# Attention's diagonal term summed by TensorE from transposed k and r, with loads and weight parts re-timed

## The chip, the core and the metric

One NeuronCore of a Trainium2 chip runs the whole program. Its engines are PE (TensorE: matmuls and, as "PEld", the weight loads that go with them), DVE (VectorE), ACT (ScalarE), POOL (GpSimd) and SP (SyncE, which here issues nearly all DMAs). Each works off its own list of instructions in order and waits for others by semaphores. PE writes only to PSUM; DVE and ACT read PSUM. The metric is the device time of one execution in microseconds (us); lower is better.

## What is computed

An RWKV-like attention over 4 batches, 8 heads, 768 steps and 48 dimensions per head, and then a mixture of experts (8 experts, top 2) over the 3072 tokens that it yields. The part that the change touches is the attention:

```python
def _attn_ref(r, k, v, w, u):
    state = np.zeros((B, H, D, D), dtype=np.float32)
    for t in range(S):
        kt, vt, rt = (k[:, :, t], v[:, :, t], r[:, :, t])
        cur = np.einsum('bhd,bhe->bhde', u[None] * kt, vt)
        y[:, :, t] = np.einsum('bhd,bhde->bhe', rt, state + cur)
        state = w[None, :, :, None] * state + np.einsum('bhd,bhe->bhde', kt, vt)
```

The term with `cur` is, for each token and head, one number c = sum over d of r·u·k, times that token's v. Below it is the "u-term", and c is the tile `c8` (128 tokens by 8 heads).

## The kernel before

**Tiles.** The attention is cut into 24 tiles (`NT`) of 128 tokens: six chunks of time by four batches, batch innermost. One loop runs over the tiles i = 0 to 23; the expert part follows and has its own loops. The order of each engine's instructions is the order in which the Python code writes them (a manual schedule), so software pipelining is written by hand: iteration i of the loop finishes tile i and prepares tiles i+1 and i+2.

**One iteration.** POOL multiplies k by powers of w (`prep_k`, two halves of four heads, tile `kd`), and for the u-term r by k (`uterm_rk`) and the product by u (`uterm_u`, tile `rku`); it also scales the state (`zup_p`). PE multiplies keys with values (`kvup`, into `RV`), then builds the output in `yout`: from tile 4 on the state's part (`zb`), the router logits of tile i-1, and the masked scores `am` times v, all into one PSUM tile `py`. Next PE turns k and r of tile i+2 (`turn_kr`, into `KX` and `RV`), computes the scores of tile i+1 into `PAB`, and turns the finished output of tile i (`turn_x`). DVE reads `kvup`'s result (`zup_v`, tile `zt`), sums `rku` over d into `c8` (`uterm_b`), adds y and c·v into `x` (`xout`), scales the turned r (`rT`), and masks the scores (`mask`, two halves). ACT copies the turned k (`kT`), the turned x (`xT`), the state (`zb`) and the logits (`lg`), and, from tile 9 on, multiplies v by c head by head (`uterm_c`: `CV_EARLY` heads an iteration early, the rest in its own); up to tile 8 DVE does that in one instruction (`cv`).

**Between these** stand two more streams. `one_step` puts one or two small DVE instructions of the router (from iteration 8 on) at eight places of an iteration. And the first expert's weights (`w_split`) come in seven parts: a load of 512 or 384 KB into a staging tile `stg`, two ACT copies that round it (lines 344 and 347) and two DVE subtractions that keep the rest (lines 346 and 349). `W_LD` says at the end of which iteration a part is loaded, `W_AT0` from which iteration on it is split (three iterations each).

**Loads.** k and r of a tile are loaded six iterations ahead, v five ahead, all from SP, which also stores every x and loads the weight parts, in the order of the code. Buffers: 3 for `kd`, 6 each for k, r, v, 4 for x; one PSUM bank for `py`.

Two dependencies follow from the whole-tile bookkeeping of `py`: `lg` waits for the last matmul written to `py` before it in the code, and `xout` waits for `lg`.

Of the kernel before, what the change touches and what calls it, by code (L numbers as in the profile page):

```python
# [9 lines left out]
F32 = mybir.dt.float32  # L10
# [5 lines left out]
AF = mybir.ActivationFunctionType  # L16
# [12 lines left out]
XD2 = 4  # L29
FILL = 1  # L30
PVB = 4
CV_EARLY = 3
STEPS_P1 = 0.8
STEPS_P2 = 4.2
STEPS_R = 1.6
# [4 lines left out]
NK = 6  # L40
# [3 lines left out]
W_AT = ((3, 7, 8), (3, 5, 7, 9))  # L44
NOT = 4

W_LD = {1: 0, 3: 1, 5: 2, 7: 3, 9: 4, 11: 5, 14: 6}
W_AT0 = (4, 6, 8, 11, 13, 16, 18)


@with_exitstack
def kernel(
# [83 lines left out]

    per_dim(wp, w, (nc.sync, nc.scalar))
    per_dim(up, u, (nc.scalar, nc.scalar))
    kd = [att.tile([128, H, 64], F32, name=f"kd{j}", bufs=1) for j in range(3)]
    rd = [att.tile([128, H, 64], F32, name=f"rd{j}", bufs=1) for j in range(NK)]  # L140
    rt, kt, vt = {}, {}, {}

    def load(i, part=(0, 3)):
        c, b = divmod(i, B)
        for nm, src, dst in (("kt", k, kt), ("rt", r, rt), ("vt", v, vt))[part[0]:part[1]]:
            if nm == "rt":
                t = rd[i % NK][:, :, :D]
# [7 lines left out]
    load(0, (0, 2))  # L155
    load(1, (0, 2))
    load(0, (2, 3))
    ub = att.tile([128, H, D], F32, name="ub", bufs=1)
    load(2, (0, 1))
    load(1, (2, 3))  # L160
    load(2, (1, 3))
# [47 lines left out]
    nc.vector.tensor_mul(pwk[:, :, 96:128], pwk[:, :, 64:96], pwk[:, :, 95:96].to_broadcast([128, NP, 32]))  # L209
    nc.scalar.activation(pwr[:, :, 0:64], pwk[:, :, 127:63:-1], AF.Copy)  # L210
    w128 = const.tile([128, NP, 1], F32, name="w128")

    kT, rT = {}, {}
    def turn_rows(dst, o, src, base=0):
# [27 lines left out]
    pub = psum.tile([128, H, 64], F32, name="pub", tag="py0")
    for p in range(NP):
        nc.tensor.transpose(pub[:, 2 * p:2 * p + 2, :].rearrange("p a b -> p (a b)"),
                            up[:, p:p + 1].to_broadcast([128, 128]), ident)
    nc.scalar.activation(ub, pub[:, :, :D], AF.Copy)
# [133 lines left out]


    AM, X, CV, PY, PA = {}, {}, {}, {}, {}
    LG, XT, PL = {}, {}, {}

    KD = {}
    HALVES = (slice(0, H // 2), slice(H // 2, H))

    def prep_k(i):
        KD[i] = kd[i % 3][:, :, :D] if i else att.tile([128, H, D], F32, name="rku")
        for h in HALVES:  # L390
            nc.gpsimd.tensor_mul(KD[i][:, h], kt[i][:, h], tabk[:, h, :D])  # L391

    RKU, C8 = {}, {}

    def uterm_rk(i):
        RKU[i] = att.tile([128, H, D], F32, name="rku")
        for h in HALVES:
            nc.gpsimd.tensor_mul(RKU[i][:, h], rt[i][:, h], kt[i][:, h])

    def uterm_u(i):  # L400
        for h in HALVES:
            nc.gpsimd.tensor_mul(RKU[i][:, h], RKU[i][:, h], ub[:, h])

    def uterm_a(i):
        uterm_rk(i)
        uterm_u(i)

    def uterm_b(i):
        c8 = att.tile([128, H, 1], F32, name="c8", bufs=2)
        nc.vector.tensor_reduce(c8, RKU[i], AX.X, ALU.add)  # L410
        C8[i] = c8
        CV[i] = att.tile([128, H, D], F32, name="cv")
        if i <= GROUPS[0][1]:
            nc.vector.tensor_mul(CV[i], vt[i], c8.to_broadcast([128, H, D]))
# [6 lines left out]
    def turn_kr(i):  # L421
        if i >= NT:
            return
        for src, dst in ((kd[i % 3], KX), (rd[i % NK], RV)):
            for p in range(NP):
                turn_rows(dst, p * 64, pair(src, p))
        kT[i] = att.tile([128, NP, 128], F32, name="kT", bufs=2)
        nc.scalar.activation(by_row(kT[i]), halves_of(KX, 0, NP), AF.Copy)
        rT[i] = att.tile([128, NP, 128], F32, name="rT", bufs=2)
        nc.vector.tensor_mul(by_row(rT[i]), halves_of(RV, 0, NP), by_row(pwr))  # L430
        one_step()
# [58 lines left out]
    def yout(i):  # L490
        c, b = divmod(i, B)
        pyb = psum.tile([128, 512], F32, name="py", tag="py0")
        PL[i - 1] = pyb[:, DM:DM + LREP * 2 * E].rearrange("p (a e) -> p a e", e=2 * E)
        py = pyb[:, :DM].rearrange("p (h d) -> p h d", d=D)
        first = [True, True]

        def acc_mm(o, lhsT, rhs, q, last):
            qs = slice(q * 64, (q + 1) * 64)
            nc.tensor.matmul(o[qs], lhsT[:, qs], rhs, start=first[q], stop=last, skip_group_check=True)  # L499
            first[q] = False  # L500

# [619 lines left out]
    def tick():  # L1121
        for x in late_mm:
            x[0] -= 1
            if x[0] == 1:
                x[2]()
        while late_mm and late_mm[0][0] <= 0:
            late_mm.pop(0)[1]()
            credit[0] -= 0.25
        at_pe[0] = max(at_pe[0] - 1, 0)

    def one_step():
        k = 0
# [12 lines left out]

    consts_a()
    uterm_rk(0)
    prep_k(1)
    prep_k(0)
    uterm_u(0)  # L1150
    scores(0)
    mask(0)
    load(4)
    load(5, (0, 2))
    warm(WARM3)
    turn_kr(1)
    uterm_b(0)
    nc.vector.tensor_mul(w128, tmpw[:, :, 63:64], tmpw[:, :, 63:64])
    def rstep(us, lag=2):

# [53 lines left out]
                          zrow[:96, None, :].to_broadcast([96, 2, DM]))  # L1214

    def products(i):
        if i + 2 < NT:
            prep_k(i + 2)
        zup_p(i - 1)
        if i + 1 < NT:  # L1220
            uterm_a(i + 1)

    flag = consts_c()
    for i in range(NT):
        products(i)
# [315 lines left out]
```

## Time and profile before

| | |
|---|---|
| Time, median of 3 runs (lowest to highest) | 593.28 us (592.33 to 593.3) |
| The profiled execution, its own time | 594.2 us |
| Its span, first to last instruction | 592.5 us |
| Mean granted TensorE clock | 0.993 |
| PE busy over the span | 565.8 us (96%) |
| DVE, ACT, POOL busy | 359.4, 286.5, 274.0 us |

The profiled execution is 0.9 us above the median and has 1.7 us outside its span. In the slices of the page PE is busy nearly without a break in the expert part, from about 133 us on, where no line of the change runs; the first 133 us are the attention, where PE, DVE and the DMA queues are all busy between 80 and 100% and hand work to each other tile by tile.

### The profile page before, as it was taken

Reading aid. Unit: us, or ns where it says so; the run is one execution under the profiler, and the core shown is the slowest. Engines: PE = TensorE matmul, PEld = TensorE weight load, DVE = VectorE, ACT = ScalarE, POOL = GpSimd, SP = SyncE. Lnnn points to the kernel's source line nnn. Section 1 sums busy time; section 2 is a strip of 40 time slices with the busy share of each in tenths; the row PEclk is TensorE's granted clock in tenths of the full one; section 3 lists DMA queues with packets and bytes.
Section 4 is the critical chain, followed back from the end, with each engine's and each line's share of the span. In section 5 each row is a group of like instructions: output and inputs, shape, how many; then the busy total and the mean of one; then the engine's idle time right before and its main releaser. Section 6 shows DMA issues by size and latency. Waiting matters only on the chain.

```text
span 592.5 us, 13758 instructions
## 1 busy us (share of the span) xinstructions
PE 565.8 (96%) x5281; PEld 540.4 (91%) x5282; DVE 359.4 (61%) x866; ACT 286.5 (48%) x721; POOL 274.0 (46%) x420
## 2 busy tenths in 40 slices
PE   7897987889999999999999999999999999999995
PEld 5897886879999999999999999999999999999995
DVE  5998998977886554546455645555454546454331
ACT  4456786853362633554445554454545454445220
POOL 8987876721015543426333552344242526333222
PEclk9899999999999999999999999999999999999999
DMA  9989999429514643874655645464845555423211
GB/s 149 192 204 191 225 209 196 102 70 267 182 60 146 203 143 84 194 173 152 140 168 113 198 114 175 102 181 111 198 129 159 153 134 174 124 93 84 66 35 42
DMA packets 143016, 86.44 MB, mean 146 GB/s; under 512 B 118415, under 2 KB 133006, under 8 KB 142944
## 3 DMA queue, kind: packets, MB, share of 16 engines
q1 hardware_dynamic: 132384, 56.67, 40.6%
q0 software_dynamic: 9936, 28.83, 15.9%
q8 instruction: 43, 0.70, 0.5%
q14 instruction: 29, 0.24, 0.1%
q10 hardware_dynamic: 624, 0.00, 0.1%
HBM read 58.83 MB, written 19.76 MB: 133 GB/s over the span
## 4 chain that ended last, share of the span: by engine, by line
PE 79%; DVE 10%; DMA 5%; ACT 2%; POOL 2%; issue 2%; POOLq 0%; SPq 0%; ACTq 0%
PE ph L1044 35%; PE pym L1078 33%; PE py L499 2%; PE pym L1069 2%; PE pym L1071 2%; DVE am L451 2%; DMA stg<-in_moe_w_dram 2%; DVE x L518 2%; DVE rT L430 1%; DMA xg<-xd,GR 1%; DMA out_dram<-ot,TK 1%; PE KX L217 1%; DVE c L410 1%; PE py L527 1%; PE PAB L443 1%
## 5 line engine op out<-in xcount | busy, mean ns | idle before, releaser
L1078 PE MATMUL pym<-w1h,hb 128*128 128x384 f32 x768 | 200.6, 337 | 0.0
L1048 DVE SCALAR_TENSOR_TENSOR hb<-ph,hb 128x384 fp32r<-128x384 f32 (+1 forms) x136 | 72.5, 533 | 116.3 <-ACT ht L1046 68.4
L1044 PE MATMUL ph<-xh,w0h 128*128 128x384 f32 (+3 forms) x408 | 140.0, 344 | 0.0
L1078 PEld LDWEIGHTS pym<-w1h,hb 128*128 128x128 f32 x768 | 139.4, 188 | 0.3
L1044 PE MATMUL ph<-xh,w0l 128*128 128x384 f32 (+3 forms) x408 | 138.8, 341 | 0.0
L1044 PE MATMUL ph<-xl,w0h 128*128 128x384 f32 (+3 forms) x408 | 133.5, 341 | 0.0
L1078 PE MATMUL pym<-w1l,hb 128*128 128x384 f32 x384 | 129.5, 337 | 0.0
L1046 ACT ACTIVATE hb<-ph 128x384 fp32r<-128x384 f32 (+1 forms) x136 | 64.2, 472 | 107.7 <-PE ph L1044 105.0
L1101 POOL DMA_INDIRECT out_dram<-ot,TK x56 | 58.8, 1050 | 103.6 <-DVE ot L1097 52.6
L947 POOL DMA_INDIRECT xg<-xd,GR x56 | 61.2, 1092 | 70.6 <-DVE r_oa L636 18.8
L1044 PEld LDWEIGHTS ph<-xh,w0h 128*128 128x128 f32 x408 | 76.7, 188 | 3.3 <-ACT xh L987 0.2
L1044 PEld LDWEIGHTS ph<-xh,w0l 128*128 128x128 f32 x408 | 76.7, 188 | 2.6
L1044 PEld LDWEIGHTS ph<-xl,w0h 128*128 128x128 f32 x408 | 76.1, 188 | 2.8
L1078 PEld LDWEIGHTS pym<-w1l,hb 128*128 128x128 f32 x384 | 72.1, 188 | 0.1
L956 POOL DMA_INDIRECT pv<-out_dram,GA x49 | 49.8, 1016 | 48.2 <-DMA out_dram<-ot,TK 35.8
L1018 ACT ACTIVATE xh<-xj 128x384 fp32r<-128x384 f32 (+1 forms) x42 | 21.1, 502 | 43.5 <-DVE xj L1016 41.6
L1086 ACT ACTIVATE ot<-pym 128x384 f32<-128x384 f32 x39 | 19.0, 486 | 40.6 <-PE pym L1078 29.9
L1019 DVE TENSOR_TENSOR xl<-xj,xh 128x384 fp32r<-128x384 f32 (+1 forms) x42 | 22.4, 534 | 24.7 <-ACT xh L1018 13.6
L1004 ACT ACTIVATE pl<-xg 128x768 uint16<-128x768 uint16 (+1 forms) x42 | 35.3, 841 | 1.0 <-DMA xd<-pl 0.9
L391 POOL TENSOR_TENSOR kd<-kt,tabk 128x192 f32<-128x192 f32 x46 | 27.7, 624 | 12.8 <-PE RV L463 6.4
L451 DVE TENSOR_TENSOR am<-PAB,mneg 128x512 int32<-128x512 int32 x48 | 31.6, 680 | 1.9 <-PE PAB L443 1.8
L419 ACT ACTIVATE cv<-vt,c 128x48 f32<-128x48 f32 x120 | 30.2, 323 | 5.0 <-DVE c L410 2.6
(272 smaller groups left out, 827.3 us busy)
## 6 DMA issues: line engine op xcount, KB each, us to landing
stg<-in_moe_w_dram SPq DMA_DIRECT2D x24, 512.0 KB
stg<-in_moe_w_dram SPq DMA_DIRECT2D x32, 384.0 KB
rd<-in_r_dram SPq DMA_DIRECT2D x24, 192.0 KB
vt<-in_v_dram SPq DMA_DIRECT2D x24, 192.0 KB
xd<-x SPq DMA_DIRECT2D x24, 192.0 KB
out_dram<-ot SPq DMA_DIRECT2D x16, 288.0 KB
kt<-in_k_dram SPq DMA_DIRECT2D x23, 192.0 KB
xg<-xd,GR POOLq DMA_INDIRECT x56
```

The lines of the kernel that those rows point to most:

```text
L391: nc.gpsimd.tensor_mul(KD[i][:, h], kt[i][:, h], tabk[:, h, :D])
L419: nc.scalar.activation(CV[i][:, h, :], vt[i][:, h, :], AF.Copy, scale=C8[i][:, h, :])
L451: nc.vector.tensor_tensor(am[:, :, h].bitcast(I32), pa[:, :, h].bitcast(I32), mneg[:, None].to_broadcast([128, 2, NP // 2, 128]), op=ALU.b ...
L947: nc.gpsimd.indirect_dma_start(out=xg[:n], out_offset=None, in_=xd[:rows_of(early_)], in_offset=bass.IndirectOffsetOnAxis(ap=GR[:n, e * NJ ...
L956: nc.gpsimd.indirect_dma_start(out=pv[:n], out_offset=None, in_=out, in_offset=bass.IndirectOffsetOnAxis(ap=GA[:n, e * NJ + t:e * NJ + t + ...
L1004: nc.scalar.activation(pl[:n], XG[e, t][:n, :DM].bitcast(U16).rearrange("p (d two) -> p two d", two=2), AF.Copy)
L1019: nc.vector.tensor_sub(xl, xj, xh.bitcast(F32))
L1044: nc.tensor.matmul(ph[:, :w_], a[:, d, fs], x[:, d, :w_], start=(j == 0), stop=(j == len(q) - 1))
L1046: nc.scalar.activation(h_[:, f, 0, :], ph[:, a:b], AF.Relu)
L1048: nc.vector.scalar_tensor_tensor(h_[:, f, 1, :], ph[:, a:b], 0.0, h_[:, f, 0, :].bitcast(F32), op0=ALU.max, op1=ALU.subtract)
L1078: nc.tensor.matmul(py, hb[:, f, a, hs], x[:, f, :], start=(j == 0), stop=(j == len(q) - 1))
L1101: st = nc.gpsimd.indirect_dma_start(out=out, out_offset=bass.IndirectOffsetOnAxis(ap=TK[:n, q:q + 1], axis=0), in_=ot[:n], in_offset=None, ...
```

## The change

The u-term is computed from the transposed tiles instead. POOL multiplies `rT` by `kT` (128 partitions of two heads' dimensions, 4 pairs of heads by 128 tokens, two halves of 256 elements), and PE sums over the partitions: eight matmuls per tile with two columns each, whose moving operand is `uw`, a table of u times w by heads. The sum lands in a free corner of the PSUM tile `py`, and DVE copies its 8 columns to `c8`. The multiplication by u on POOL and the sum on DVE go, and with them the table `ub`.

```diff
-CV_EARLY = 3
+CV_EARLY = 2
+NKD = 4
-W_LD = {1: 0, 3: 1, 5: 2, 7: 3, 9: 4, 11: 5, 14: 6}
-W_AT0 = (4, 6, 8, 11, 13, 16, 18)
+W_LD = {1: 0, 4: 1, 6: 2, 9: 3, 11: 4, 14: 5, 16: 6}
+W_AT0 = (5, 8, 10, 13, 15, 18, 20)
...
     def uterm_a(i):
-        uterm_rk(i)
-        uterm_u(i)
-
-    def uterm_b(i):
-        c8 = att.tile([128, H, 1], F32, name="c8", bufs=2)
-        nc.vector.tensor_reduce(c8, RKU[i], AX.X, ALU.add)
-        C8[i] = c8
+        RK[i] = att.tile([128, NP, 128], F32, name="rk", bufs=2)
+        for h in (slice(0, NP // 2), slice(NP // 2, NP)):
+            nc.gpsimd.tensor_mul(RK[i][:, h], rT[i][:, h], kT[i][:, h])
+
+    def uterm_sum(i, pyb, alone):
+        c8 = pyb[:, CO:CO + H].rearrange("p (a s) -> p a s", s=2)
+        for p in range(NP):
+            for q in range(2):
+                qs = slice(q * 64, (q + 1) * 64)
+                nc.tensor.matmul(c8[qs, p, :], RK[i][:, p, qs], uw[:, p, :], start=alone, stop=True,
+                                 skip_group_check=True)
+        C8[i] = att.tile([128, H, 1], F32, name="c8", bufs=2)
         CV[i] = att.tile([128, H, D], F32, name="cv")
+        return lambda: nc.vector.tensor_copy(C8[i][:, :, 0], pyb[:, CO:CO + H])
+
+    def uterm_v(i):
         if i <= GROUPS[0][1]:
-            nc.vector.tensor_mul(CV[i], vt[i], c8.to_broadcast([128, H, D]))
+            nc.vector.tensor_mul(CV[i], vt[i], C8[i].to_broadcast([128, H, D]))
...
     def products(i):
-        if i + 2 < NT:
-            prep_k(i + 2)
-        zup_p(i - 1)
         if i + 1 < NT:
             uterm_a(i + 1)
+        zup_p(i - 1)
+        if i + 3 < NT:
+            prep_k(i + 3)
...
-        if i + 6 < NT:
-            load(i + 6, (0, 2))
+        if i + 5 < NT:
+            load(i + 5, (0, 2))
...
         yout(i)
+        if i + 1 < NT:
+            c8_out = uterm_sum(i + 1, PB[i], False)
...
-        if i + 5 < NT:
-            load(i + 5, (2, 3))
+        if i + 4 < NT:
+            load(i + 4, (2, 3))
...
         one_step()
         one_step()
+        uterm_v(i)
+        xout(i)
         if i + 1 < NT:
-            uterm_b(i + 1)
+            c8_out()
         one_step()
-        one_step()
-        xout(i)
         one_step()
...
             mask(i + 1)
             tick()
             one_step()
+            one_step()
```

On PE, at tile 4, the first with `zb` (names as in the text; `L499` with `zb` and with `am` and `L527` are `yout`, `L217` the turns, `L443` the scores, `L463` `kvup`), before:

```order
L463 MATMUL RV<-vt,kd_100 48x48 x8
L499 MATMUL py<-zb_212,rT 64x96 x8
L527 MATMUL py<-wg,xT 64x64 x6
L499 MATMUL py<-vt,am 64x48 x16
L217 MATMUL KX<-ident,kd_99 128x64 x8
L217 MATMUL RV<-ident,rd_102 128x64 x8
L443 MATMUL PAB<-rT,kT 128x128 x8
L217 MATMUL KX<-ident,x 128x64 x6
```

and after the change:

```order
L462 MATMUL RV<-vt,kd_99 48x48 x8
L499 MATMUL py<-zb_211,rT 64x96 x8
L527 MATMUL py<-wg,xT 64x64 x6
L499 MATMUL py<-vt,am 64x48 x16
L405 MATMUL py<-uw,rk 64x2 x8
L218 MATMUL KX<-ident,kd_101 128x64 x8
L218 MATMUL RV<-ident,rd_103 128x64 x8
L442 MATMUL PAB<-rT,kT 128x128 x8
L218 MATMUL KX<-ident,x 128x64 x6
```

The eight matmuls of the sum (`L405`) stand between `yout` and the turns, so everything behind them on PE comes later by their length, and they are now the last writes to `py` before `lg`.

On DVE, at tile 10 (`L410` is the sum over d, `L518` x, the lines `RT`, `r_d`, `r_s` are router steps, `w0l` a weight part's rest), before:

```order
L451 TENSOR_TENSOR am<-PAB,mneg 128x2x256
L561 SCALAR_TENSOR_TENSOR RT<-RT,r1r 128x64
L346 TENSOR_TENSOR w0l_505<-stg,w0h_504 128x512
L476 TENSOR_TENSOR zt<-RV,z_210 128x192
L561 SCALAR_TENSOR_TENSOR RT<-RT,r1r 128x64 x2
L410 TENSOR_REDUCE c_1434<-rku 128x8
L561 SCALAR_TENSOR_TENSOR RT<-RT,r1r 128x64
L563 SCALAR_TENSOR_TENSOR RT<-RT,r1s 128x64
L518 TENSOR_TENSOR x<-py,cv 128x384
L703 TENSOR_SCALAR RT<-RT 128x64
L430 TENSOR_TENSOR rT<-RV,pwr 128x2x4x64
```

and after the change:

```order
L450 TENSOR_TENSOR am<-PAB,mneg 128x2x256
L561 SCALAR_TENSOR_TENSOR RT<-RT,r1r 128x64 x2
L346 TENSOR_TENSOR w0l_519<-stg,w0h_518 128x512
L475 TENSOR_TENSOR zt<-RV,z_209 128x192
L561 SCALAR_TENSOR_TENSOR RT<-RT,r1r 128x64 x2
L518 TENSOR_TENSOR x<-py,cv 128x384
L409 COPY c_1483<-py 128x8
L563 SCALAR_TENSOR_TENSOR RT<-RT,r1s 128x64
L703 TENSOR_SCALAR RT<-RT 128x64
L429 TENSOR_TENSOR rT<-RV,pwr 128x2x4x64
```

x moved ahead of two router steps and of c; c is a copy of 8 columns behind it.

On POOL, from iteration 5 on (numbers at the end of a name are buffers; `L391` is `prep_k`, `L398` r times k, `L402` times u, `L480` the state), before:

```order
L391 TENSOR_TENSOR kd_100<-kt,tabk 128x4x48 x2
L480 TENSOR_TENSOR z_208<-zt,w_172 128x192
L398 TENSOR_TENSOR rku<-rd_102,kt 128x192 x2
L402 TENSOR_TENSOR rku<-rku,ub 128x192 x2
L391 TENSOR_TENSOR kd_101<-kt,tabk 128x4x48 x2
```

and after the change:

```order
L398 TENSOR_TENSOR rk<-rT,kT 128x256 x2
L479 TENSOR_TENSOR z_207<-zt,w_173 128x192
L391 TENSOR_TENSOR kd_99<-kt,tabk 128x4x48 x2
L398 TENSOR_TENSOR rk<-rT,kT 128x256 x2
L479 TENSOR_TENSOR z_208<-zt,w_173 128x192
```

One pair of multiplications is gone, the other is a third longer and reads what DVE and ACT wrote, not the loads.

## Rows read from the trace of the kernel before

**Rows 1.** Stretches: length, PE, PEld, DVE, ACT, POOL busy (count), clock, DMA share, GB/s.
```profile
20.02:50.54 30.52, 29.70 (x767) 27.93 (x767) 28.38 (x57) 15.70 (x39) 27.11 (x45) 0.99 0.87 188
50.54:58.13 7.59, 5.43 (x140) 5.11 (x136) 5.95 (x16) 4.45 (x15) 5.76 (x10) 1.00 1.07 230
58.13:122.94 64.81, 55.20 (x1354) 50.98 (x1354) 61.58 (x184) 48.89 (x166) 46.45 (x82) 0.97 0.77 173
122.94:133.33 10.39, 7.72 (x180) 6.65 (x176) 7.46 (x26) 6.01 (x24) 3.69 (x6) 1.00 0.27 80
133.33:592.50 459.17, 452.40 (x2627) 438.48 (x2627) 242.08 (x553) 203.51 (x464) 174.08 (x227) 1.00 0.50 139
```

**Rows 2.** Timeline, tile 9: start us, length, engine, line, tiles [idle before, releaser].
```profile
55.38 0.66 SPq L520 DMA_DIRECT2D xd<-x  x1
...
55.52 0.63 ACT L344 ACTIVATE w0h<-stg 128x512 fp32r<-128x512 f32 x1 [2.98 <-DMA stg<-in_moe_w_dram]
...
56.66 1.14 POOL L391 TENSOR_TENSOR kd<-kt,tabk 128x192 f32<-128x192 f32 x2 [1.41 <-DMA kt<-in_k_dram]
...
58.13 0.56 DVE L518 TENSOR_TENSOR x<-py,cv 128x384 f32<-128x384 f32 x1 [1.42 <-ACT lg L536]
...
58.60 0.21 DVE L556 SCALAR_TENSOR_TENSOR r1r<-RT,r1r 128x64 f32<-128x64 f32 x1
...
58.74 0.68 DVE L430 TENSOR_TENSOR rT<-RV,pwr 128x512 f32<-128x512 f32 x1
```

**Rows 3.** Timeline of PE and DVE at tiles 18 and 19.
```profile
108.04 0.68 DVE L430 TENSOR_TENSOR rT<-RV,pwr 128x512 f32<-128x512 f32 x1
...
108.78 0.44 PEld L463 LDWEIGHTS RV<-vt,kd 128*48 128x48 f32 x16 [0.37 <-DVE rT L430]
108.78 0.56 PE L463 MATMUL RV<-vt,kd 128*48 128x48 f32 x16 [0.23 <-DVE rT L430]
...
110.20 1.09 PE L499 MATMUL py<-vt,am 128*64 128x48 f32 x32
```

**Rows 4.** Groups of instructions, 15 to 133.3 us: count, busy us, mean ns, idle before.
```profile
L398 POOL TENSOR_TENSOR rku<-rd,kt 128x192 f32<-128x192 f32 x44 | 26.9, 633 | 0.0
...
L410 DVE TENSOR_REDUCE c<-rku 128x8 f32<-128x384 f32 x22 | 11.9, 541 | 0.2 <-POOL rku L402 0.2
...
L480 POOL TENSOR_TENSOR z<-zt,w 128x192 f32<-128x192 f32 x16 | 8.9, 559 | 7.4 <-DVE RT L712 1.2 <-ACT cv L419 1.1 <-DVE r_s L707 1.1
...
L536 ACT ACTIVATE lg<-py 128x16 f32<-128x16 f32 x23 | 4.1, 176 | 9.5 <-PE py L499 9.5
...
L656 PE MATMUL RT<-r_ob,r_oa 128*128 128x16 bf16 x8 | 0.4, 171 | 0.0
...
L660 DVE COPY L<-RT 128x14 f32<-128x14 f32 x1 | 0.2, 172 | 1.4 <-PE RT L656 1.4
```

**Rows 5.** Stretches, `L656` alone: length, PE busy (count), PEld, clock, DMA share, GB/s.
```profile
15.00:133.30 118.30, 0.36 (x8) 0.27 (x8) 0.97 0.79 174
```

**Rows 6.** Waits from 0 to 175 us: total us, times, longest.
```profile
POOL kd L391 <- DMA kt<-in_k_dram: 5.2, 5, 1.8
ACT w0h L344 <- DMA stg<-in_moe_w_dram: 4.6, 2, 3.0
```

**Rows 7.** Timeline of the prologue.
```profile
7.14 1.14 POOL L391 TENSOR_TENSOR kd<-kt,tabk 128x192 f32<-128x192 f32 x2
...
15.22 0.55 DVE L518 TENSOR_TENSOR x<-py,cv 128x384 f32<-128x384 f32 x1
```

**Rows 8.** Timeline of DVE, tiles 12 and 13.
```profile
73.89 0.55 DVE L518 TENSOR_TENSOR x<-py,cv 128x384 f32<-128x384 f32 x1
...
78.36 0.55 DVE L518 TENSOR_TENSOR x<-py,cv 128x384 f32<-128x384 f32 x1
```

**Rows 9.** Timeline, two weight-part subtractions, the second beside a POOL multiplication.
```profile
43.91 0.68 DVE L349 TENSOR_TENSOR w0l<-stg,w0h 128x512 fp32r<-128x512 f32 x1
...
53.15 1.09 DVE L349 TENSOR_TENSOR w0l<-stg,w0h 128x512 fp32r<-128x512 f32 x1
...
53.66 1.59 POOL L402 TENSOR_TENSOR rku<-rku,ub 128x192 f32<-128x192 f32 x2
```

More of the change, by code (lines that the diff above doesn't have):

```diff
@@ L138 @@
     per_dim(up, u, (nc.scalar, nc.scalar))
-    kd = [att.tile([128, H, 64], F32, name=f"kd{j}", bufs=1) for j in range(3)]
+    kd = [att.tile([128, H, 64], F32, name=f"kd{j}", bufs=1) for j in range(NKD)]
     rd = [att.tile([128, H, 64], F32, name=f"rd{j}", bufs=1) for j in range(NK)]
@@ L157 @@
     load(0, (2, 3))
-    ub = att.tile([128, H, D], F32, name="ub", bufs=1)
     load(2, (0, 1))
@@ L211 @@
     w128 = const.tile([128, NP, 1], F32, name="w128")
+    uw = const.tile([128, NP, 2], F32, name="uw")
     kT, rT = {}, {}
@@ L241 @@
     turn0(rd[0], rT, pwr, "rT", RV)
[L242 to L246, printed above, removed]
+    nc.vector.memset(uw, 0.0)
+    for s in range(2):
+        q = slice(s * 64, (s + 1) * 64)
+        nc.vector.tensor_mul(uw[q, :, s], up[q], wp[q])
     nc.vector.tensor_scalar(mneg[:, 0, :], idif, 0.0, -1.0, op0=ALU.is_gt, op1=ALU.mult)
@@ L256 @@
     XO, VO = NP * 64, NP * 64
+    CO = DM + LREP * 2 * E
     kvp = RV[:, 0, VO:VO + NP * D].rearrange("p (a d) -> p a d", d=D)
@@ L382 @@
     AM, X, CV, PY, PA = {}, {}, {}, {}, {}
-    LG, XT, PL = {}, {}, {}
+    LG, XT, PL, PB = {}, {}, {}, {}
     KD = {}
@@ L388, in prep_k @@
     def prep_k(i):
-        KD[i] = kd[i % 3][:, :, :D] if i else att.tile([128, H, D], F32, name="rku")
+        KD[i] = kd[i % NKD][:, :, :D] if i else att.tile([128, H, D], F32, name="cv")
         for h in HALVES:
             nc.gpsimd.tensor_mul(KD[i][:, h], kt[i][:, h], tabk[:, h, :D])
[L393 to L402, printed above, removed]
-    def uterm_a(i):
-        uterm_rk(i)
-        uterm_u(i)
-    def uterm_b(i):
-        c8 = att.tile([128, H, 1], F32, name="c8", bufs=2)
-        nc.vector.tensor_reduce(c8, RKU[i], AX.X, ALU.add)
-        C8[i] = c8
+    RK, C8 = {}, {}
+    def uterm_a(i):
+        RK[i] = att.tile([128, NP, 128], F32, name="rk", bufs=2)
[9 more added lines that the diff above has]
+        C8[i] = att.tile([128, H, 1], F32, name="c8", bufs=2)
         CV[i] = att.tile([128, H, D], F32, name="cv")
+        return lambda: nc.vector.tensor_copy(C8[i][:, :, 0], pyb[:, CO:CO + H])
+    def uterm_v(i):
         if i <= GROUPS[0][1]:
-            nc.vector.tensor_mul(CV[i], vt[i], c8.to_broadcast([128, H, D]))
+            nc.vector.tensor_mul(CV[i], vt[i], C8[i].to_broadcast([128, H, D]))
     def uterm_c(i, a, b):
@@ L423, in turn_kr @@
             return
-        for src, dst in ((kd[i % 3], KX), (rd[i % NK], RV)):
+        for src, dst in ((kd[i % NKD], KX), (rd[i % NK], RV)):
             for p in range(NP):
@@ L492, in yout @@
         pyb = psum.tile([128, 512], F32, name="py", tag="py0")
-        PL[i - 1] = pyb[:, DM:DM + LREP * 2 * E].rearrange("p (a e) -> p a e", e=2 * E)
+        PB[i] = pyb
+        PL[i - 1] = pyb[:, DM:CO].rearrange("p (a e) -> p a e", e=2 * E)
         py = pyb[:, :DM].rearrange("p (h d) -> p h d", d=D)
@@ L1146 @@
     consts_a()
-    uterm_rk(0)
     prep_k(1)
+    uterm_a(0)
     prep_k(0)
-    uterm_u(0)
+    prep_k(2)
     scores(0)
     mask(0)
-    load(4)
-    load(5, (0, 2))
+    load(4, (0, 2))
     warm(WARM3)
     turn_kr(1)
-    uterm_b(0)
+    uterm_sum(0, psum.tile([128, 512], F32, name="py", tag="py0"), True)()
     nc.vector.tensor_mul(w128, tmpw[:, :, 63:64], tmpw[:, :, 63:64])
```

## The prediction

> **What bounds the kernel now.** I read the busy time by stretch first [rows 1], cut at the starts of x of tiles 1, 8, 9 and 21 and at the first matmul of the experts. From 133.33 us on PE is busy 452.40 of 459.17 us and no edited line runs: that part can only be shifted. So the question is by how much the attention ends sooner or later. Its middle is not one stage. Tiles 2 to 8 (seven, 4.36 us each) have PE busy 29.70 of 30.52 us, 97%: PE bounds them, with DVE just behind (28.38). Tile 9 alone takes 7.59 us. Tiles 10 to 21 (twelve, 5.40 each) have DVE busy 61.58 of 64.81, 95%: the router's steps have come to DVE, which now bounds, while PE has 55.20. The last two tiles take 10.39.
>
> Next the cause of tile 9 [rows 2]: ACT stands 2.98 us before the rounding of a weight part, because its load has not landed; `lg` is queued behind that on ACT, and x waits 1.42 us for `lg`. Then the hand-over inside a tile [rows 3]: rT ends at 108.72, `kvup` (it overwrites what rT reads) starts 0.06 later, then the state's part, logits and scores times v follow without a break to 111.29. So a tile's `yout` ends 2.57 us after rT, at the earliest.
>
> **What the change costs and gives.** Prices first.
>
> The sum on PE: eight matmuls, 16 records as the trace counts them. No row has two columns. The nearest with half-width weights is `kvup`, 16 records in 0.44 (weight loads) to 0.56 us (matmuls) [rows 3]; the smallest matmuls of the trace, 16 columns, are busy for 0.36 us in eight [rows 5], of which 0.171 is the last one's own length, so 0.19/7 = 0.027 each [rows 4], some 0.43 for 16. The two halves of the array work side by side in `kvup` and in the sum alike, so 0.25 could be enough. I take 0.42, range 0.25 to 0.56. It lies between `yout` and the turns, so on PE's path in every tile, and ahead of x: `lg` waits for the last write to `py`, which was `L499` [rows 4] and is now the sum. From the end of `yout`, x can start after 0.42 + 0.18 (`lg`) + about 0.1 for two hand-overs, 0.70.
>
> The copy of c on DVE: like the copy of 14 columns, 0.17 us, against 0.54 for the sum over d [rows 4]; DVE is freed of 0.37, about 0.36 a tile.
>
> POOL: a half of 192 elements takes 0.63 us as a group's mean [rows 4], one of 256 by proportion 0.84, so `rk` takes 1.7 us. It starts when rT is done and PE wants it 2.57 us later, at the end of `yout`: 0.9 to spare, so it costs nothing as long as POOL is free then. POOL has per tile 1.25 (`kd`, as long as `L398`'s pair) + 1.7 + 0.56 for the state [rows 4] = 3.5 us, less than any period.
>
> The loads: `kd` of tile j is now queued ahead of `rk` of tile j-1, which the sum needs in iteration j-2. Before, in the stretch where POOL waits for loads (5.2 us in all [rows 6]), `kd` of tile 12 started at 56.66, ended 57.80, and rT of tile 11 started only at 58.74 [rows 2]. `kt` is now issued one iteration later, but SP runs in order and is behind the code, so what counts is what stands before it in SP's list: one x store more (its issue takes 0.66 us there [rows 2]) and at several tiles one weight part less. The cover is about 1 us.
>
> The weight parts: parts 1 and 2, the two for which ACT waits 4.6 us [rows 6], get four iterations between load and use where they had three (loaded at the end of 4 and 6, split from 8 and 10 on). In SP's list the same loads of k, r and v stand ahead of each as before, and one x store more. An iteration is worth 4 to 5 us [rows 1], so a wait of 2.98 goes. What is late next in that tile is DVE (5.95 busy [rows 1], less 0.36).
>
> Now the sum, against the profiled execution of 594.2.
> - Up to x of tile 1 (20.02 [rows 1]). POOL's queue: `kd` 1 ends at 8.3 [rows 7], `rk` 0 10.0, `kd` 0 11.1, `kd` 2 12.3, `rk` 1 14.0. PE stands before the sum of tile 1 till then, 14.2; then `kvup` 14.8, state 15.2, c·v 15.8, x of tile 0 ends at 16.4 (before: 15.77 [rows 7]), rT, mask and `yout` bring x of tile 1 to about 20.2: +0.2 (-0.5 to +0.8).
> - Tiles 2 to 8: PE-bound, 7 x 0.42 = 2.9, less the 0.8 in which PE idled: +2.1 (+0.9 to +3.1). DVE's 0.36 buys nothing here.
> - Tile 9: from 7.59 to about 5.3: -2.3 (0 if the load still comes late, -2.5 if DVE is no bound).
> - Tiles 10 to 21: at most 12 x 0.36 = 4.3 back, if DVE stays the bound. But the chain has a floor: rT's end, 2.57 to the end of `yout`, 0.70 to x, x 0.5, c 0.1, two steps at 0.21 [rows 2], rT 0.68: 5.0 a tile (4.6 for tiles 20 and 21, without `kvup`). A tile like 13, 73.89 to 78.36, 4.47 us [rows 8], gets half a us longer; one of 6 us gets 0.36 shorter. I take -1.8 (-4.3 to +0.4).
> - Last two tiles: the sum once on the path, c's 0.37 off it: +0.2.
> - Experts: 0.
>
> Together +0.2 + 2.1 - 2.3 - 1.8 + 0.2 = **-1.6**, so 592.6 for the profiled execution; the median lies 0.92 below that execution, so **591.7**.
>
> One rule is weighed beside this. DVE's subtraction of two SBUF tiles takes 0.68 us alone and 1.09 beside a POOL multiplication, which itself takes 1.59 where 1.14 is usual [rows 2, 9]. The Trainium skill, in "SBUF — State Buffer", section "SBUF: two separate sides", says that a Vector instruction with two SBUF inputs and a GpSimd instruction share one pair of ports, which the first to start holds to its end. The trace agrees. By that rule less POOL work (3.5 instead of 4.3 us a tile, a fifth) would take a fifth off the excess of the 14 subtractions, an estimate of 0.4 us: 591.3 instead of 591.7. I leave it out of the sum.
>
> **Rivals.**
> (1) The DVE release comes through whole. For it: 95% busy in tiles 10 to 21, and a sum of 0.25 would put the floor at 4.8. Against it: the light tiles already run at 4.5 to 4.9. Price: -4.3 instead of -1.8 and +0.9 instead of +2.1, in all -5.3: 588.0.
> (2) Slower: the sum makes PE and the hand-over PE, ACT, DVE the bound of the whole stage. Place: `yout`, sum, `lg`, x. It decides from about 0.55 us per sum on, the matmul length of `kvup` [rows 3]: the floor is then 5.2 and tiles 10 to 21 give nothing (+0.4), tiles 2 to 8 cost 3.1, the prologue and the last tiles 0.4 each, tile 9 gives 2.1: +2.2, 595.5.
> (3) The loads are too near: POOL waits for `kt` with `rk` queued behind it, PE waits for `rk`. It decides when `kt` lands more than 1 us later than now; three or four tiles at 1 us each: about +2.5, 595.8.
> (4) The change does not do what its re-timing says: DMA is busy 0.87 to 1.07 of the time till 58 us [rows 1], so ACT waits for the weight parts as before. Then tile 9 gives nothing: 594.0.
>
> **How the numbers follow.** Chances: forecast 0.42, (1) 0.17, (2) 0.21, (3) 0.08, (4) 0.12. About 0.2% (1.2 us) is what a measurement can tell from no change: faster is below 592.1, slower above 594.5. The forecast's own range is 589.5 to 593.5; of its 0.42, 0.25 fall below 592.1, 0.14 within, 0.03 above. With (1) that makes faster 0.43; same 0.14 + 0.09 of (4) + 0.04 of (2) = 0.27; slower 0.03 + 0.17 of (2) + 0.08 + 0.02 of (4) = 0.30. For eight in ten the range reaches from just below (1) to just above (2) and (3): 587.5 to 596.
>
> **What would show it.** In the profile after: the sum's 16 records between `yout` and the turns, about 0.4 us a tile; `lg` waiting for the sum's line; x of tile 8 about 2 us later than 50.54; no ACT wait of 3 us before a weight part; tiles 9 to 21 together some 4 us shorter than 72.4; the first expert matmul near 131.7. It would be wrong if PE waits for POOL at the sum, if POOL's waits for `kt` grow beyond 5.2 us and fall on PE, or if the expert part changes its length of 459 us.

## The result

The changed kernel takes 599.58 us (median of 4 runs, 598.97 to 600.02), the kernel before 593.1 us on the same chip: a ratio of 1.0111, with a 95% interval from 1.0093 to 1.0128. It is slower by 1.1%, outside the forecast range of 587.5 to 596.0, and on the other side of the forecast of 591.7.

The span of the profiled execution went from 592.5 to 598.1 us, +5.6. The first view is the same one that the prediction began with [rows 1]: busy time by stretch, cut at the starts of x of tiles 1, 8, 9 and 21 and at the first matmul of the experts, in the changed kernel (columns: stretch, length, then PE, PEld, DVE, ACT, POOL busy with counts, clock, DMA share, GB/s).

```profile
20.64:53.19 32.55, 32.24 (x891) 31.19 (x887) 26.56 (x57) 15.28 (x38) 22.03 (x33) 1.00 0.90 192
53.19:58.81 5.62, 5.62 (x152) 5.46 (x148) 4.21 (x12) 4.39 (x15) 3.44 (x6) 1.00 1.02 244
58.81:129.32 70.51, 59.56 (x1536) 54.99 (x1532) 58.51 (x184) 48.69 (x166) 37.79 (x57) 1.00 0.70 157
129.32:139.15 9.83, 9.00 (x211) 8.10 (x207) 9.02 (x30) 6.89 (x26) 3.56 (x4) 1.00 0.28 85
139.15:598.10 458.95, 452.46 (x2627) 438.13 (x2627) 242.37 (x554) 203.66 (x464) 175.03 (x227) 1.00 0.49 139
```

Against the stretches of before, with the prediction's term beside each:

| stretch | before | after | difference | predicted |
|---|---|---|---|---|
| up to x of tile 1 | 20.02 | 20.64 | +0.6 | +0.2 |
| tiles 2 to 8 | 30.52 | 32.55 | +2.0 | +2.1 |
| tile 9 | 7.59 | 5.62 | -2.0 | -2.3 |
| tiles 10 to 21 | 64.81 | 70.51 | **+5.7** | **-1.8** |
| last two tiles | 10.39 | 9.83 | -0.6 | +0.2 |
| experts | 459.17 | 458.95 | -0.2 | 0 |

Five of the six terms came out within a microsecond of what was written. One is wrong by 7.5 us, more than the 7.2 us by which the span missed (+5.6 for -1.6). In that stretch PE is busy 59.56 of 70.51 us and DVE 58.51: neither bounds it any more, nor does ACT (48.69) or POOL (37.79). Something makes them wait for each other, 0.5 us more in each of twelve tiles where 0.15 less was forecast.

The timeline of one such tile shows it, tile 15 of the changed kernel (start, length, engine, line, output<-input; in brackets idle time before it and what ended it).

```profile
89.20 0.68 DVE L429 TENSOR_TENSOR rT<-RV,pwr 128x512 f32<-128x512 f32 x1
...
90.05 1.42 POOL L398 TENSOR_TENSOR rk<-rT,kT 128x256 f32<-128x256 f32 x2 [2.92 <-DVE RT L563]
...
91.36 1.09 PE L499 MATMUL py<-vt,am 128*64 128x48 f32 x32
...
91.43 0.51 POOL L479 TENSOR_TENSOR z<-zt,w 128x192 f32<-128x192 f32 x1
...
91.97 0.74 ACT L486 ACTIVATE zb<-z 64x192 f32<-64x192 f32 x2 [1.49 <-POOL z L479]
...
92.28 0.60 PE L405 MATMUL py<-uw,rk 128*64 128x2 f32 x16
...
92.72 1.46 ACT L418 ACTIVATE cv<-vt,c 128x48 f32<-128x48 f32 x6
...
94.09 0.16 ACT L536 ACTIVATE lg<-py 128x16 f32<-128x16 f32 x1
...
94.28 0.56 DVE L518 TENSOR_TENSOR x<-py,cv 128x384 f32<-128x384 f32 x1 [0.79 <-DMA rd<-in_r_dram]
```

Read it as a chain: rT ends at 89.88, POOL multiplies `rk` until 91.47, and only then the state, `z`, until 91.94; ACT stands 1.49 us for `z`, copies it to `zb` until 92.71, then scales six heads of v by c until 94.18; x starts at 94.28. PE had finished `yout` at 92.45 and the sum at 92.88. x could have started about 1.1 us sooner, and the next rT waits behind x. (The releaser named beside x, a load, had landed long before; by the end times it is ACT's `lg`, which stands right behind the last `cv` and ends 0.07 us after it.) In all of tiles 9 to 20 x starts 0.10 us after the last `cv` ends.

The waits of the changed kernel from 0 to 175 us show the same in sums (total us, times, longest):

```profile
ACT zb L486 <- POOL z L479: 22.7, 16, 2.3
POOL rk L398 <- DVE rT L429: 13.4, 9, 2.3
DVE x L518 <- ACT lg L536: 12.2, 16, 1.5
ACT lg L536 <- PE py L405: 8.5, 8, 1.8
POOL kd L391 <- DMA kt<-in_k_dram: 2.6, 3, 1.2
```

The first line is new: `zb` never waited for `z` by anything to speak of before, and now all 16 tiles that have a `z` do.

Why is it new? Before, POOL's order was `kd`, `z`, then r times k: `kd` and r times k read loaded data, `z` the `zt` of the tile before, and POOL ran ahead of the chain. The same tile, 15, in the kernel before:

```profile
86.26 0.72 ACT L487 ACTIVATE zb<-z 64x192 f32<-64x192 f32 x2
...
87.01 1.24 ACT L419 ACTIVATE cv<-vt,c 128x48 f32<-128x48 f32 x5
...
87.99 0.51 POOL L480 TENSOR_TENSOR z<-zt,w 128x192 f32<-128x192 f32 x1 [0.83 <-DVE GTS L783]
...
88.15 0.16 ACT L536 ACTIVATE lg<-py 128x16 f32<-128x16 f32 x1
...
89.65 0.54 DVE L518 TENSOR_TENSOR x<-py,cv 128x384 f32<-128x384 f32 x1
```

`zb` has no wait there, and the `z` that POOL makes at 87.99 is already the one for the next tile's `zb`. The change put `rk` first, and `rk` needs rT, the end of the chain; `z`, ready since the tile before, stands behind it in POOL's queue, and `zb` stands ahead of the `cv` pieces in ACT's. So a state that is needed only three tiles later came to hold up the x of this tile.

### The profile page after: what moved, and what is told of

It reads as the page before. It is cut to its first block, busy times and chain, and to the rows that moved or that the text cites. A ratio compares the mean times of both kernels' runs of the same rounds, so it can differ in the third digit from the quotient of the medians.

```text
span 598.1 us, 14501 instructions
## 1 busy us (share of the span) xinstructions
PE 576.0 (96%) x5661; PEld 550.8 (92%) x5662; DVE 353.3 (59%) x869; ACT 286.1 (48%) x720; POOL 255.8 (43%) x373
## 4 chain that ended last, share of the span: by engine, by line
PE 73%; DMA 2%; DVE 1%; POOL 1%; issue 1%; ACT 0%; POOLq 0%
PE ph L1044 35%; PE pym L1078 32%; PE pym L1069 2%; PE pym L1071 2%; DMA xg<-xd,GR 1%; DMA out_dram<-ot,TK 1%; POOL xg L947 1%; PE ptm L970 0%; PE RT L656 0%; PE py L499 0%; DVE x L518 0%; POOL rk L398 0%; DVE am L450 0%; ACT cv L418 0%; PE KX L218 0%
## 5 line engine op out<-in xcount | busy, mean ns | idle before, releaser
L1048 DVE SCALAR_TENSOR_TENSOR hb<-ph,hb 128x384 fp32r<-128x384 f32 (+1 forms) x136 | 72.4, 532 | 117.6 <-ACT ht L1046 72.2
L947 POOL DMA_INDIRECT xg<-xd,GR x56 | 62.5, 1116 | 67.7 <-DVE r_oa L636 17.8
L1044 PEld LDWEIGHTS ph<-xl,w0h 128*128 128x128 f32 x408 | 76.1, 188 | 3.0
L398 POOL TENSOR_TENSOR rk<-rT,kT 128x256 f32<-128x256 f32 x48 | 34.2, 735 | 44.5 <-DVE rT L429 13.4
L391 POOL TENSOR_TENSOR kd<-kt,tabk 128x192 f32<-128x192 f32 x46 | 31.1, 697 | 5.3 <-DMA kt<-in_k_dram 2.6
```

The source lines that it names most:

```text
L398: nc.gpsimd.tensor_mul(RK[i][:, h], rT[i][:, h], kT[i][:, h])
L947: nc.gpsimd.indirect_dma_start(out=xg[:n], out_offset=None, in_=xd[:rows_of(early_)], in_offset=bass.IndirectOffsetOnAxis(ap=GR[:n, e * NJ ...
L1044: nc.tensor.matmul(ph[:, :w_], a[:, d, fs], x[:, d, :w_], start=(j == 0), stop=(j == len(q) - 1))
L1048: nc.vector.scalar_tensor_tensor(h_[:, f, 1, :], ph[:, a:b], 0.0, h_[:, f, 0, :].bitcast(F32), op0=ALU.max, op1=ALU.subtract)
```

## The experiments

Twelve kernels ran, four at a time, each four on one chip with the kernel before beside them. Its median there was 595.6 to 595.9 us, some 2.5 above the first measurement, so the ratios are what is compared. Theory A is the chain just read: POOL's order makes `z`, `zb`, `cv` and x late. Its rivals are B, that six `cv` pieces (one head of c times v each) within the iteration are simply one too many for ACT, and C, that the sum on PE with the hand-over behind it bounds x.

**z ahead of rk.** Only the order of POOL's multiplications:

```diff
-        if i + 1 < NT:
-            uterm_a(i + 1)
         zup_p(i - 1)
+        if i + 1 < NT:
+            uterm_a(i + 1)
```

> The changed kernel, but POOL multiplies the state (z) ahead of r times k instead of behind it; nothing else moves. Theory A, POOL's order: after rT, POOL does rk (1.42 us), then z (0.51), ACT then zb (0.74) and six c-times-v pieces (1.46), and only then x can start; z is ready before rT, so put ahead it costs rk little, ACT gets zb and the pieces done about 1.4 us sooner, and tiles 10 to 21 go from 70.5 to about 62 us (5.2 a tile, where the sum's hand-over to lg bounds): 599.6 becomes 591.5, between 590 and 593. Theory B, six c-times-v pieces where there were five are what is too long on ACT: no gain over 1 us, since all six stay. Theory C, the sum on PE (0.60 us a tile instead of 0.42) and the hand-over behind it bound x: no gain, 599 to 600.

Measured: 591.24 us, ratio 0.9932 (0.9904 to 0.9959). One line moved, and a kernel 1.1% slower than before is 0.7% faster than it. The timeline of the same tile, 15, in this kernel:

```profile
87.11 0.69 DVE L429 TENSOR_TENSOR rT<-RV,pwr 128x512 f32<-128x512 f32 x1
...
87.94 1.43 POOL L398 TENSOR_TENSOR rk<-rT,kT 128x256 f32<-128x256 f32 x2 [1.12 <-DVE RT L563]
...
88.70 0.72 ACT L486 ACTIVATE zb<-z 64x192 f32<-64x192 f32 x2
...
89.27 1.09 PE L499 MATMUL py<-vt,am 128*64 128x48 f32 x32
...
89.44 1.47 ACT L418 ACTIVATE cv<-vt,c 128x48 f32<-128x48 f32 x6
...
90.19 0.60 PE L405 MATMUL py<-uw,rk 128*64 128x2 f32 x16
...
90.83 0.18 ACT L536 ACTIVATE lg<-py 128x16 f32<-128x16 f32 x1
...
91.05 0.56 DVE L518 TENSOR_TENSOR x<-py,cv 128x384 f32<-128x384 f32 x1
```

`zb` has no wait, and from rT's start to x it takes 3.94 us where it took 5.08. Now the end of the sum releases `lg`, and that x: 0.69 us after `yout`, the 0.70 of the prediction. Tiles 9, 10, 13, 14 and 19 show the same; in 11, 12 and 16 to 18 `lg` is done 0.4 to 1.1 us sooner and DVE is busy up to x. The stretches of this kernel, tiles 2 to 8, tile 9, tiles 10 to 21:

```profile
20.70:54.11 33.41, 32.07 (x881) 30.93 (x879) 25.36 (x56) 15.03 (x37) 21.42 (x33) 1.00 0.88 183
54.11:60.31 6.20, 6.20 (x138) 6.07 (x134) 3.97 (x13) 4.42 (x14) 3.59 (x7) 0.72 1.03 250
60.31:122.28 61.97, 58.38 (x1561) 55.52 (x1556) 57.52 (x184) 49.91 (x166) 36.58 (x57) 1.00 0.80 179
```

Tiles 10 to 21 take 61.97 us: 2.8 less than before, where 1.8 was forecast. That term was sound but for the chain it left out.

**zb behind the turned x.** POOL's order stays as the change has it; ACT copies the state later:

```diff
         if i:
-            zblock(i - 1)
             uterm_c(i, CV_EARLY, H)
...
             turn_x(i)
+            if i:
+                zblock(i - 1)
             mask(i + 1)
```

> The changed kernel with POOL's order kept (rk ahead of z), but ACT's copy zb moved behind the turned x's copy, so that neither the c-times-v pieces nor lg are queued behind it. If theory A is right in that the late z hurts only through ACT's queue, this gains as much as z ahead: 591 to 593. If POOL's lateness itself hurts (rk late for the sum, kd late), it stays near 599; under B about 599 (six pieces stay); under C 599 to 600.

Measured: 589.67 us, ratio 0.9918 (0.9894 to 0.9943). Its stretches, cut in the same way:

```profile
20.62:53.44 32.82, 31.96 (x885) 30.96 (x881) 26.55 (x56) 14.88 (x37) 21.27 (x32) 1.00 0.85 183
53.44:58.26 4.82, 4.82 (x144) 4.74 (x140) 4.08 (x13) 4.32 (x15) 2.81 (x5) 1.00 0.86 240
58.26:119.50 61.24, 57.64 (x1556) 55.20 (x1551) 56.97 (x184) 51.15 (x168) 38.86 (x59) 1.00 0.84 190
```

`z` is as late here as in the changed kernel (in tile 15 of both it ends 2.06 us after rT), and the loss is gone all the same. So POOL's lateness hurts only by way of ACT's queue: the cause is the pair, `z` behind `rk` and `cv` behind `zb`, and breaking either link is enough.

**Three early pieces.** `CV_EARLY` back from 2 to 3, in the changed kernel, and then together with z ahead of rk.

```diff
-CV_EARLY = 2
+CV_EARLY = 3
```

> The changed kernel with three of the eight c-times-v pieces an iteration early again, so five instead of six in their own. Theory A (POOL's order delays zb, the pieces stand behind it): one piece of 0.24 us less behind the late zb in each of 12 tiles, -2.9 us, about 596.7, and x still waits for ACT's last piece. Theory B (the number of pieces): most of the loss returns, about 593 to 594. Theory C (the sum's length): no change, 599.5.

> z ahead of rk, and three pieces early. Theory A: with z ahead the pieces end before lg does, so the third early piece adds nothing: equal to z ahead alone within 0.7 us. Theory B: the gain is that of the three early pieces, about 593, whatever POOL does. If both matter, some 1 to 3 us below z ahead alone.

Measured: alone 598.29 us, ratio 1.0049 (1.0028 to 1.0069); with z ahead 590.76 us, 0.9923 (0.9895 to 0.9951). Alone it shortens the chain by a piece, as theory A has it, and does not break it; the tile timeline of that kernel still has `zb` waiting and x after the last piece:

```profile
91.16 0.74 ACT L486 ACTIVATE zb<-z 64x192 f32<-64x192 f32 x2 [1.31 <-POOL z L479]
91.91 1.24 ACT L418 ACTIVATE cv<-vt,c 128x48 f32<-128x48 f32 x5
93.06 0.16 ACT L536 ACTIVATE lg<-py 128x16 f32<-128x16 f32 x1
...
93.25 0.56 DVE L518 TENSOR_TENSOR x<-py,cv 128x384 f32<-128x384 f32 x1 [0.57 <-ACT lg L536]
```

With z ahead the third piece adds nothing that can be measured. The number of pieces is not the cause, though with the chain in place each one costs.

**The sum twice.** z ahead of rk, and the eight matmuls done a second time into columns that nobody reads, ahead of the true ones:

```diff
-        c8 = pyb[:, CO:CO + H].rearrange("p (a s) -> p a s", s=2)
-        for p in range(NP):
+        for o in (CO + H, CO):
+            c8 = pyb[:, o:o + H].rearrange("p (a s) -> p a s", s=2)
+            for p in range(NP):
...
```

> z ahead of rk, and the sum on PE done twice (the first into columns that nobody reads), so PE has 16 more records a tile ahead of lg. If the sum lies on the path from yout to x in nearly every tile (x starts 0.69 us after yout in half of them), 22 tiles cost 0.5 to 0.6 us each: +11 to +13, about 603. If DVE bounds tiles 9 to 21 and only tiles 2 to 8 follow PE, +4 to +6, about 596. If PE has room, under +2.

Measured: 602.11 us, ratio 1.0119 (1.0071 to 1.0166), against 0.9932 with one sum, though that ran on another chip: 0.0187 of 595.8, or 11.1 us. In the trace x starts 1.16 us after the end of `yout` where it was 0.69, so the second sum costs 0.47; and x follows 0.26 us after the end of the sum in 18 of tiles 1 to 21, against 13 with one sum. So once the chain on ACT is gone, a sum costs what it is long in most tiles: it is on the path yout, sum, `lg`, x. (In tiles 11, 16 and 17 DVE is busy up to x all the same.) The 11.1 us spread over 24 sums are 0.46 each, but that this equals the 0.47 is partly chance: the profile with two sums also has 3.5 us in which PE stands with nothing that the profile names (last section), the one with one sum none marked so. In the records a double sum is busy 1.06 us where one is 0.60:

```profile
57.64 1.06 PE L406 MATMUL py<-uw,rk 128*64 128x2 f32 x32
...
58.75 0.18 ACT L537 ACTIVATE lg<-py 128x16 f32<-128x16 f32 x1 [2.03 <-PE py L406]
58.97 0.56 DVE L519 TENSOR_TENSOR x<-py,cv 128x384 f32<-128x384 f32 x1 [0.88 <-ACT lg L537]
```

**The weight parts alone, in the kernel before, and undone.** First the two tables of the change in the kernel before, nothing else; later the tables of before in the kernel with `zb` behind:

```diff
-W_LD = {1: 0, 3: 1, 5: 2, 7: 3, 9: 4, 11: 5, 14: 6}
-W_AT0 = (4, 6, 8, 11, 13, 16, 18)
+W_LD = {1: 0, 4: 1, 6: 2, 9: 3, 11: 4, 14: 5, 16: 6}
+W_AT0 = (5, 8, 10, 13, 15, 18, 20)
```

> The kernel before with one part of the change alone: the two tables that say when a weight part is loaded and split. Theory: this part alone is worth what tile 9 gains, since the 3 us wait of ACT before a weight part goes: -2.0 us against before, ratio 0.9965. Rival, the DMA queues are full there and the wait only moves: within 0.5 us of before. A second rival: the last parts are now split in iterations 18 to 22, beside the router's steps, which takes back 1 us: ratio 0.998.

> zb behind the turned x, with the weight parts loaded and split when the kernel before does. If the re-timing acts here as it did in the kernel before (-2.0 us there), the ACT wait before a part comes back and it costs +2 against the anchor. Rival: it was worth something only together with the old order; within 0.7 us of the anchor.

Measured: in the kernel before 593.5 us, ratio 0.9966 (0.9949 to 0.9983), the -2.0 that was forecast. Its tile 9 takes 5.13 us instead of 7.59, and the rounding of the part, which ACT had waited 2.98 us for [rows 2], starts with no wait:

```profile
52.87 0.62 ACT L344 ACTIVATE w0h<-stg 128x512 fp32r<-128x512 f32 x1
```

Undone in the kernel with `zb` behind: 592.22 us, ratio 0.9957 (0.9932 to 0.9981), against 0.9946 (0.9919 to 0.9973) for the anchor on that chip. No difference can be told, and among its waits up to 175 us there is none of ACT for a part's load. With the rest of the change in place the re-timing earns nothing more. Why isn't shown: tiles 2 to 8 are some 2 us longer with the sum, and loads of k, r and v are issued an iteration later; either may let a part loaded by the old table land in time.

**c copied by ACT.** With `zb` behind, the copy of c's eight columns moved from DVE to ACT; the anchor is that kernel without the move, once more.

```diff
-        return lambda: nc.vector.tensor_copy(C8[i][:, :, 0], pyb[:, CO:CO + H])
+        return lambda: nc.scalar.activation(C8[i][:, :, 0], pyb[:, CO:CO + H], AF.Copy)
```

> The kernel with zb behind the turned x once more, as the anchor for the three others on the same chip. Theory A: again a ratio of 0.992 to before, within 0.989 to 0.995.

> zb behind the turned x, and the copy of c's 8 columns done by ACT instead of DVE. If DVE bounds tiles 9 to 21 with zb out of the way, the 0.15 us of the copy come off 13 tiles: -1 to -2 against the anchor. If the path yout, sum, lg, x bounds them, no change (within 0.7 us); if ACT is short of time, +1.

Measured: anchor 593.02 us, ratio 0.9946 (0.9919 to 0.9973); c on ACT 593.53 us, 0.9976 (0.9955 to 0.9997). No gain; if anything a loss, but the intervals overlap. In the profiles tiles 4 to 8 take 4.84 to 4.96 us with it, where the first run with `zb` behind has 4.64 to 4.73 in tiles 4 to 7: the copy stands ahead of the turned k on ACT, which may be why.

**Farther loads.** k and r six iterations ahead and v five, as before the change: with z ahead of rk; with z ahead and `zb` behind; and with `zb` behind alone, next to the anchor.

```diff
-        if i + 5 < NT:
-            load(i + 5, (0, 2))
+        if i + 6 < NT:
+            load(i + 6, (0, 2))
...
-        if i + 4 < NT:
-            load(i + 4, (2, 3))
+        if i + 5 < NT:
+            load(i + 5, (2, 3))
```

> z ahead of rk as before, and the loads put back to six iterations ahead for k and r and five for v, as in the kernel before the change. Theory L, the loads are too near: with z ahead, POOL waited 10.6 us in seven places for k, once 3.6 us, with rk queued behind, and tiles 8 and 9 took 6.25 and 6.20 us where their neighbours take 4.65 and 4.9; farther loads give back some 2 to 3 us: 588.5. Rival, DMA traffic: the loads land late because the DMA engines are busy until 58 us, not because they are issued late; no gain, 591.2 within 1 us, or x stores and weight parts behind the loads land later.

> z ahead of rk, ACT's copy zb behind the turned x, and the farther loads. If the three act on different waits: z ahead gives nothing more once zb is out of the way, and farther loads give 1 to 3 us: 587 to 588.5. If they meet the same bound (the sum's hand-over to lg and DVE), the same as zb behind alone, 589.7 within 1 us.

> zb behind the turned x, with k and r loaded six and v five iterations ahead. If the farther loads are what made the two earlier kernels with them 595 (they ran on another chip than those without), +3 to +4 against the anchor here. If it was the chip and the chance of a run, within 1 us. If the nearer loads do harm (theory L), -1 to -3.

Measured: 595.1 us, 0.9990 (0.9964 to 1.0016); 594.98 us, 0.9984 (0.9958 to 1.0009); 594.76 us, 1.0002 (0.9981 to 1.0022). The first two ran on another chip than their counterparts; the third ran beside its anchor and is above it by 1.7 us in the median, 2.8 in the mean and 0.56% in the ratios, whose intervals are apart. So the farther loads cost some 2 to 3 us, and the theory that the nearer ones hurt is wrong, although the waits of POOL for k that it started from were there (11.3 us with z ahead, 5.0 with the farther loads). What they cost is not explained: the profiled execution of the third is, by chance, the lowest of its 11 times (592.52) and that of the anchor the highest of its 11 (594.36), and the attention ends 1.2 us sooner in the former. Over all runs the mean granted clock was 0.9898 with the farther loads and 0.9931 in the anchor, which goes the same way as the times but does not say what lowers it. This stays open.

## Why the prediction was wrong

The step that failed is the one on POOL: `rk` "costs nothing as long as POOL is free then", backed by a sum of POOL's work per tile, 3.5 us, "less than any period". `rk` itself was in time (in tile 15 it ended at 91.47, `yout` at 92.45). The step counted how much POOL does and when `rk` is wanted, and took the state as a length in a sum. It didn't ask what is queued behind `rk` on POOL, who waits for that, and what is queued behind the waiter on ACT, although the document shows the new order, `rk`, `z`, `kd`, in its fence for POOL. It did ask this of `kd` and the loads, rival (3), and so had the right question on the wrong neighbour. With it, the working was at hand: rT's end + 1.7 + 0.56 + `zb` 0.72 + six `cv` at 0.25 = 4.5 us to x, against 2.57 + 0.70 by way of `yout`, so ACT is the later by more than a microsecond. With x, c, two steps and rT itself, 1.7 us in the prediction's floor, that is some 6 us a tile where a mean of 5.9 was measured and 5.0 stood in the prediction. (The lengths of `zb` and `cv` were in the trace of before, as in its tile 15 above.)

Point by point:

- The sum's price, 0.42 on the path: right. The group of records is 0.60 us long, above the range, but it overlaps its neighbours: from the end of `yout` to the next turn PE takes 0.36 (tile 7 after) where the two overlapped by 0.06 before (tile 15), and the second sum of the experiment cost 0.47.

```profile
46.54 1.09 PE L499 MATMUL py<-vt,am 128*64 128x48 f32 x32
...
47.46 0.60 PE L405 MATMUL py<-uw,rk 128*64 128x2 f32 x16
...
47.99 0.46 PE L218 MATMUL KX<-ident,kd 64*128 64x64 f32 x8
```

```profile
86.95 1.09 PE L499 MATMUL py<-vt,am 128*64 128x48 f32 x32
...
87.98 0.47 PE L217 MATMUL KX<-ident,kd 64*128 64x64 f32 x8
```

- From the end of `yout` to x, 0.70: right, 0.69 wherever the sum ends last.
- Tiles 2 to 8, +2.1: right (+2.0). Tile 9, -2.3: right (-2.0), the wait for the weight part gone.
- Tiles 10 to 21, -1.8: wrong as the change stands (+5.7). With either link of the chain broken it is -2.8 or -3.6, between the forecast and rival (1).
- c's copy: 0.155 us instead of 0.54, and DVE's busy time in tiles 10 to 21 falls from 61.58 to 58.51. The release was real; nothing in the changed kernel could use it.
- Rival (2), slower by 595.5, had the right sign and the wrong place: it looked for the loss between the sum, `lg` and x. In the changed kernel ACT did `lg` late because of `cv`, not because of the sum.
- Rival (3): POOL's waits for k fell, from 5.2 to 2.6 us, in the changed kernel. With z ahead of rk they rose to 11.3 in the one profile, 3.6 at once, and tiles 8 and 9 lost about 3 us there; the kernel was faster all the same.
- Rival (4): the wait for the weight part did go.
- The signs that "What would show it" named for the first stages came true; the two for the later ones did not (tiles 9 to 21 took 76.1 us, not some 4 less than 72.4, and the first expert matmul came at 139.15, not near 131.7). Of the signs that it named for a failure none appeared: PE waited for POOL at the sum 1.0 us in all, POOL for loads less than before, and the expert part kept its length. The list had no line for ACT, and the loss was there.

One more estimate went astray. The 14 subtractions of the weight parts took 10.2 us before, and in the changed kernel

```profile
L346 DVE TENSOR_TENSOR w1l<-stg,w1h 128x384 fp32r<-128x384 f32 x4 | 4.2, 1058 | 0.0
...
L349 DVE TENSOR_TENSOR w1l<-stg,w1h 128x384 fp32r<-128x384 f32 x4 | 2.9, 728 | 0.0
L346 DVE TENSOR_TENSOR w0l<-stg,w0h 128x512 fp32r<-128x512 f32 x3 | 2.7, 912 | 0.0
L349 DVE TENSOR_TENSOR w0l<-stg,w0h 128x512 fp32r<-128x512 f32 x3 | 2.5, 846 | 0.0
```

12.3 us, although POOL has less to do. The Trainium skill, in "SBUF — State Buffer", section "SBUF: two separate sides", has the two engines holding one pair of ports in turn; from that I had taken that less POOL work means shorter subtractions, 0.4 us. The rule isn't contradicted, the inference is: what counts is whether a subtraction falls beside a POOL multiplication, as 12 of the 14 now do and 8 did before (91.46, 0.90 us long, beside `z` and `kd` in tile 15), and not how much POOL works in all. More than half of the 2.1 us is one of them, at 131.90 beside `rk`: 1.74 us, where the same form beside no POOL instruction takes 0.55.

## What to carry to other kernels

When an engine's queue is given an instruction that waits for the end of the chain, list everything that was ahead of the chain and now stands behind it, and follow each one through the next engine's queue to the place where the chain picks it up again; an engine with time to spare says nothing about that. If something is ready early and wanted late, issue it ahead of the instruction that waits; if something is wanted late, keep its consumer off the queue of what is wanted now. A change that loses may be a good one with two lines in the wrong order: here the same work, reordered, is 0.7 to 0.8% faster than before on one chip and 0.5% on another (0.9932, 0.9918; 0.9946), and these versions beat both kernels.

## What the runs showed of the hardware

PE stood still within one group of matmuls, with all operands there and nothing in the profile to end it, for about 1 us. This is tile 7 of the anchor kernel (`zb` behind, its second run), where `yout` is in the middle of its scores:

```profile
47.38 0.74 PE L499 MATMUL py<-vt,am 128*64 128x48 f32 x20
49.09 0.56 PE L499 MATMUL py<-vt,am 128*64 128x48 f32 x12 [0.97 <-issue]
```

The tile took 5.81 us, against 4.64 in the profile of the first run of the same kernel. Such stops come at other tiles in other runs.

The packets in the trace point to a cause, though no run tests it. There is a DMA queue of kind "instruction", q8, with packets of 16384 bytes, some 5 us apart in the attention. The kernel before has 43 of them, the changed one 46 and the one with the sum twice 49; three more go each time with 760 or 768 more records of PE and its weight loads: 253 to 256 records a packet, so these look like PE's own instructions. Here such a packet ended at 47.57, and PE went on 1.52 us later. In all the profiles ten stops of PE in the attention are of 0.36 us or more with nothing named that ends them; each ended 1.30 to 1.70 us after the end of a q8 packet. (One of 0.31 us came 2.89 after.) So PE seems to have waited for instructions that came late.

The granted clock early in the program also differs between runs of one kernel. From 15 to 20 us PE is busy nearly throughout in both of these rows, the first from the anchor, the second from the first run of the same kernel:

```profile
15.00:20.00 5.00, 5.00 (x86) 4.86 (x84) 4.17 (x12) 1.09 (x2) 2.77 (x5) 0.53 0.99 184
```

```profile
15.00:20.00 5.00, 4.91 (x110) 4.69 (x110) 4.67 (x12) 1.09 (x2) 3.18 (x6) 0.78 0.90 167
```

A mean of 0.53 is nearly all at the lower of the two levels, 1.2 GHz; tile 1 took 5.54 us there and 4.46 in the other. In the run with z ahead of rk the clock fell to a mean of 0.72 in tile 9 (the row 54.11:60.31 above), right after tile 8, in which PE was idle for 1.03 of 6.25 us, 0.67 of it for the `rk` that POOL made late after 3.62 us of waiting for a load of k. Tile 9 took 6.20 us with PE busy throughout, against 4.82 at a clock of 1.00 in the first run with `zb` behind. A wait can so be paid a second time in the tile behind it, but need not be: after the stop of 0.97 us above, the next tile took 4.64 us at a clock of 1.00. In the experiments with 7 to 11 runs the runs of one kernel spread over 3 to 6 us (588.77 to 594.36 in the anchor), which is as much as the whole change was worth.
